# Block-sparse attention with a token and channel mixer: landing times of the build-time planner reset, and crossbar transposes of Q and K from pair 8 on

## The chip, the core and the metric

The kernel runs on one core of one Trainium2 chip. The metric is the device time of one execution in microseconds (us). Executions of one kernel differ (the kernel before took 272.06 to 276.02 us in one session), so each time is given as a median of several runs with its range, and kernels are compared on the same chip in the same rounds. A run more than 1.5% above the fastest of its kernel counts as slow and is left out of the ratios. "Faster" or "slower" needs 2%; smaller differences are read from their 95% interval. The span is the time from the first to the last instruction in the profile. The mean clock is the share of TensorE's full clock that was granted over it.

## The reference

Four batches of eight heads, 768 positions of 64 numbers each, pass through attention under a block mask. The result, 4 x 768 x 512, passes through a mixer with one token layer and one channel layer. The code is shortened.

```python
def _attn_ref(q, k, v, sampled_blocks):            # block 32, window 1, 3 random blocks per row
    scores = scale * np.matmul(q, k.transpose(0, 1, 3, 2))
    mask = ...                                     # window | first and last block | sampled_blocks
    scores = np.where(mask, scores, -1000000000.0)
    attn = np.exp(scores - np.max(scores, axis=-1, keepdims=True))
    attn = attn / (np.sum(attn, axis=-1, keepdims=True) + 1e-09)
    return np.matmul(attn, v)

def _moe_ref(x, w_tok1, w_tok2, w_ch1, w_ch2):     # 768->256->768, then 512->1536->512
    h = np.maximum(x.transpose(0, 2, 1) @ w_tok1, 0.0) @ w_tok2
    u = x + h.transpose(0, 2, 1)
    return u + np.maximum(u @ w_ch1, 0.0) @ w_ch2
```

## The kernel before

The 32 heads are worked off as 16 pairs. For each pair, Q and K must stand transposed in `qtb` and `ktb` (head dimension on the partitions; 24 more partitions carry the mask). TensorE makes scores, ScalarE takes exponentials (`et`), TensorE multiplies by V (`po`), VectorE normalises. The token and channel matmuls fill what is left of TensorE.

**The planner.** Which instruction goes where in each engine's program is decided when the kernel is built. A `Planner` simulates the engines with a fixed cost for each operation and a landing time for each transfer; at each step an engine is given the ready operation of best priority. On the chip every engine then executes in exactly that order. A wrong landing time is therefore not a slower plan: it is an instruction in the wrong place, at which the engine stands with everything behind it.

```python
    dma = {"free": 0.0}
    RATE = 200.0

    def landing(issue, nbytes):
        dma["free"] = max(dma["free"], issue + 1.6 * US) + nbytes / RATE
        return Ev(dma["free"] + 0.6 * US)
```

From V of pair 0 on, all loads of Q, K, V and weights are issued by GpSimd, in a software queue that casts f32 to bf16; each load waits for its raw buffer (four each).

**Two ways to transpose.** Pairs below `NPE` (except pair 0, which has its own code) use TensorE: for each of K and Q a VectorE copy, six transposes, and two copies out of PSUM, the memory that TensorE writes to. Pairs from `NPE` on use the DMA's crossbar, which transposes while it moves data: VectorE copies raw K and Q into a "wide" buffer, and SyncE issues one DMA transpose for each. There are `NL` = 2 wide buffers for each of K and Q, so the copy of pair p may only go when the transpose of pair p-2 has read its buffer.

```python
    # relayout(p), for K and Q
            if nm != "v" and p >= NPE:
                deps.append(wide_there[nm, p % NL])
                if p - NL >= NPE:
                    deps.append(xb_done[nm, p - NL])        # the wide buffer is free again
            lays[nm + "ev"] = P.op(("dve",), {"dve": 320.0}, deps, emit, prio=2 if nm != "v" else 3)
    ...
    # crossbar(p), for K and Q
                nc.sync.dma_start_transpose(out=bufs[p % NV]..., in_=wide[nm, p % NL]...)
            ...
            ev = P.op(("sp",), {"sp": 1600.0}, deps, emit, prio=1, lat=5000.0)
            xb_done[nm, p] = ev                             # planned: 1.6 + 5.0 + 0.05 us
```

The softmax here doesn't subtract the row's maximum and nothing guards it: scores larger than these inputs give would overflow.

Of the kernel before, what the change touches and what calls it, by code (L numbers as in the profile page):

```python
# [25 lines left out]
def free(base_ap: bass.AP, extra_offset: int, dims) -> bass.AP:  # L26

    return bass.AP(
        tensor=base_ap.tensor,
        offset=base_ap.offset + extra_offset,  # L30
        ap=[list(base_ap.ap[0])] + [list(d) for d in dims],
    )
# [137 lines left out]
def kernel(  # L170
# [12 lines left out]
    nc = tc.nc  # L183
# [7 lines left out]
    NV = 4  # L191
    NR = 4
    NET = 8
    NPE = 10
    NL = 2

    sb1 = ctx.enter_context(tc.tile_pool(name="sb1", bufs=1))
# [12 lines left out]
    qtb = [sb1.tile([128, 2, S], BF16, name=f"qtb{n}") for n in range(NV)]  # L210
# [3 lines left out]
        for n in range(NL) for nm in ("k", "q")  # L214
    }

    P = Planner({"ps": 2, "po": 1, "pm": 3, "et": NET, "a_t": 2, "o": 3, "rc": 2,
                 "uT": 3})
    US = 1e3


    raws, arrive = {}, {}
    dma = {"free": 0.0}
    RATE = 200.0

    def landing(issue, nbytes):
        dma["free"] = max(dma["free"], issue + 1.6 * US) + nbytes / RATE
        return Ev(dma["free"] + 0.6 * US)

    def load_pair(p, t, parts=("k", "q", "v")):  # L230
        for nm, src in (("k", k), ("q", q), ("v", v)):
# [39 lines left out]
    R = slice(64, 88)  # L271
# [32 lines left out]
    for i in range(8):  # L304
# [5 lines left out]
        out=ind[R, :, :], in_=free(one[R, 0:1], 0, [[0, NC], [0, 128]]), compare_op=ALU.is_ge,  # L310
# [3 lines left out]
        out=ind[R, :, :], in_=ind[R, :, :], compare_op=ALU.is_ge, fill=0.0,  # L314
# [3 lines left out]
        out=ident[:, :], in_=free(one[:, 0:1], 0, [[0, 128]]), compare_op=ALU.is_equal, fill=0.0,  # L318
# [21 lines left out]
        out=edge[R, :], in0=edge[R, :], scalar1=-11.5, scalar2=None, op0=ALU.add  # L340
# [3 lines left out]
        out=edge[R, :], in0=edge[R, :], scalar1=121.0, scalar2=None, op0=ALU.is_gt  # L344
    )
    nc.vector.tensor_scalar(
        out=bandg[R, :], in0=dkf[R, :], scalar1=1.0, scalar2=edge[R, 0:1],
# [5 lines left out]
    for col, other in ((0, bandg), (2, allow), (4, allow)):  # L353
        nc.vector.scalar_tensor_tensor(
            out=allow[R, :], in0=kbf[R, :], scalar=sampf[R, col : col + 1], in1=other[R, :],
# [3 lines left out]
        out=t2add[R, :], in0=allow[R, :], scalar1=-MASKVAL, scalar2=MASKVAL,  # L359
# [17 lines left out]
    def first_turn(nm, hf):  # L377
        t = psM.tile([128, 3, 128], BF16, tag="pm", name=f"t{nm}first{hf}")
        for c in range(3):
            nc.tensor.matmul(  # L380
                out=t[:, c, :], lhsT=lay0[nm][:, 3 * hf + c, :, :].rearrange("p h d -> p (h d)"),
                rhs=ident[:, :], start=(c == 0), stop=(c == 2), is_transpose=True,
            )
        return t

    def first_evac(copy, nm, hf, hd, t):
        buf = (ktb if nm == "k" else qtb)[0]
        copy(
            out=buf[0:64, hd, 384 * hf : 384 * hf + 384],
            in_=t[64 * hd : 64 * hd + 64, :, :].rearrange("p c s -> p (c s)"),  # L390
        )

    def e2_mm(hf, pool, tag):
        t = pool.tile([128, 512], FP32, tag=tag, name=f"pm_e2_{hf}")
        nc.tensor.matmul(
            out=t[R, 0:384], lhsT=t2add[R, :], rhs=indf[:, 384 * hf : 384 * hf + 384],
            start=True, stop=True,
        )
        return t

    def e2_copy(copy, hf, hd, t):
        copy(out=qtb[0][R, hd, 384 * hf : 384 * hf + 384], in_=t[R, 0:384])
# [24 lines left out]
    rows_there = {p: Ev(START) for p in range(NV)}  # L427
# [3 lines left out]
    def first_rest():  # L431

        def band(eng):
            nc.vector.tensor_copy(out=ktb[0][R, 1, 384:S], in_=indf[:, 384:S])

        P.op(("dve",), {"dve": 250.0}, [], band, prio=0)
        for nm in ("k", "q"):
            box, last, rel = {}, Ev(), Ev()

            def emit(nm=nm, box=box, rel=rel):  # L440
                P.take("pm", rel)
                box["t"] = first_turn(nm, 1)

            yield 330.0, [Ev(START + (200.0 if nm == "k" else 600.0))], [("pm", 1)], emit, last
            for hd in range(2):
                def evac(eng, nm=nm, hd=hd, box=box):
                    first_evac(vcopy, nm, 1, hd, box["t"])

                ev = P.op(("dve",), {"dve": 350.0}, [last], evac, prio=0)
                f_there[nm, 1].same_as = ev  # L450
                rel.same_as = ev
        box, last, rel = {}, Ev(), Ev()

        def emit():
            P.take("pm", rel)
            box["t"] = e2_mm(1, psM, "pm")

        yield 330.0, [], [("pm", 1)], emit, last
        for hd in range(2):
            def copy(eng, hd=hd, box=box):  # L460
                e2_copy(vcopy, 1, hd, box["t"])

            e2_there = P.op(("dve",), {"dve": 420.0}, [last], copy, prio=0)
            rel.same_as = e2_there
        rows_there[0] = e2_there
        for n in range(1, NV):
            def spread(eng, n=n):
                nc.sync.dma_start(out=qtb[n][R, :, :], in_=qtb[0][R, :, :])

            rows_there[n] = P.op(("sp",), {"sp": 100.0}, [e2_there], spread, prio=0, lat=2500.0)  # L470

    def wide_stream():

        box, done, rel = {}, Ev(), Ev()

        def emit():
            P.take("pm", rel)
            box["m"] = psM.tile([128, 2, NC, 24], FP32, tag="pm", name="pm_wide")
            for i, rhs in enumerate((ident[R, 64:88], t2add[R, :])):
                for c in range(NC):  # L480
                    nc.tensor.matmul(
                        out=box["m"][:, i, c, :], lhsT=ind[R, c, :], rhs=rhs,
                        start=(i == 0 and c == 0), stop=(i == 1 and c == NC - 1),
                    )

        yield 500.0, [Ev(62 * US)], [("pm", 1)], emit, done
        for n in range(NL):
            for i, nm in enumerate(("k", "q")):
                def clear(eng, nm=nm, n=n):
                    nc.vector.memset(wide[nm, n][:, :, :, 64:128], 0.0)  # L490

                def copy(eng, nm=nm, n=n, i=i):
                    nc.vector.tensor_copy(
                        out=wide[nm, n][:, :, :, 64:88],
                        in_=free(box["m"][:, i, 0, :], 0, [[0, 2], [24, NC], [1, 24]]),
                    )
                ev = P.op(("dve",), {"dve": 420.0}, [Ev(60 * US)], clear, prio=6)
                ev = P.op(("dve",), {"dve": 450.0}, [done, ev], copy, prio=6)
                wide_there[nm, n].same_as = ev
                rel.same_as = ev  # L500
# [13 lines left out]
    def relayout(p):  # L514
        lays = {}
        for nm in ("k", "q", "v") if p else ("v",):
# [3 lines left out]
            def emit(eng, nm=nm, raw=raw):  # L520
                if nm == "v":
                    nc.vector.tensor_copy(out=vaug[p % NV][:, :, :, 0:64], in_=raw[:, :, :, :])  # L522
                elif p >= NPE:
                    nc.vector.tensor_copy(out=wide[nm, p % NL][:, :, :, 0:64], in_=raw[:, :, :, :])
# [8 lines left out]
            if nm == "v" and p >= NV:  # L533
                deps.append(pv_done[p - NV])
            if nm != "v" and 2 <= p < NPE:
                deps.append(qT_there[p - 1, 1])
# [3 lines that stand above are left out]
                    deps.append(xb_done[nm, p - NL])  # L540
# [7 lines left out]
    def crossbar(p):  # L548

        lays = relayout(p)  # L550
        for nm, bufs, there in (("k", ktb, kT_there), ("q", qtb, qT_there)):
            def emit(eng, nm=nm, bufs=bufs):
                nc.sync.dma_start_transpose(
                    out=bufs[p % NV][:, :, :].rearrange("e h (c s) -> e (h c) s", c=NC),
                    in_=wide[nm, p % NL][:, :, :, :].rearrange("p h c e -> p (h c e)"),
                )
            deps = [lays[nm + "ev"]]
            if p >= NV:
                deps.append(qk_done[p - NV])
            ev = P.op(("sp",), {"sp": 1600.0}, deps, emit, prio=1, lat=5000.0)  # L560
            xb_done[nm, p] = ev
            there[p, 0], there[p, 1] = ev, ev

    def transposes(p):
        yield lambda: ("v", p) in raws
        if p >= NPE:
            crossbar(p)
# [52 lines left out]
    def qk_stream():  # L620
        for s in steps:
# [32 lines left out]
            else:  # L654
                deps = [e for hd in range(2) for e in (kT_there[p, hd], qT_there[p, hd])]
                if p < NPE:
                    deps.append(rows_there[p % NV])
# [273 lines left out]
    P.stream(3, tok_stream())  # L931
    P.stream(4, ch_stream())
    P.stream(-1, wide_stream())


# [55 lines left out]
```

## Time and profile before

| what | before |
|---|---|
| median of 3 runs | 273.65 us (273.64 to 275.1) |
| span of the profiled execution (timed at 272.80 us) | 271.1 us, mean clock 0.992 |
| TensorE / ScalarE / VectorE busy | 97% / 68% / 43% |
| transposes on TensorE for Q and K (L587) | 54 + 54 |
| first token matmul | 30.04 us |
| last exponential ends | 149.91 + 5.33 = 155.24 us |

The DMA row of the page's slices; one slice is 6.8 us, a digit is the busy share in tenths:

```profile
DMA  6999999998699764891300036200132002310123
GB/s 146 189 219 202 213 201 208 200 201 133 70 212 170 145 101 97 136 120 39 62 2 2 0 60 174 83 33 2 39 116 80 0 0 80 117 40 0 41 77 116
```

The DMA engines are full up to slice 9 (61 us) and reach their lowest point for some time in slice 10 (68 to 75 us, 70 GB/s). The first crossbar transpose of this kernel is issued at 72.18 us, so in or after that gap.

### The profile page before, as it was taken

What the parts mean: (1) busy time and instruction counts of PE and PEld (TensorE: products, weight loads), DVE (VectorE), ACT (ScalarE), POOL (GpSimd) and SP (SyncE); (2) the same over time, 40 slices, a digit from 0 to 9 for tenths busy, and PEclk for the clock granted to TensorE, in tenths of its full rate; (3) what the DMA queues carried; (4) which work ended last, traced back from release to release, by engine and by line L of the source; (5) the groups of instructions that cost most, each with busy time, mean ns of one, the idle gap of its engine ahead of it and who ended that gap; (6) DMA issues with size and microseconds to landing.
All of it is one profiled execution on the core that took longest, in us unless ns stands there. A gap on an engine that the chain in (4) does not pass through costs nothing.

```text
span 271.1 us, 6192 instructions
## 1 busy us (share of the span) xinstructions
PE 263.4 (97%) x2587; PEld 171.5 (63%) x2595; DVE 117.8 (43%) x268; ACT 185.1 (68%) x274; POOL 42.2 (16%) x66
## 2 busy tenths in 40 slices
PE   8899999999999999999999999999999999999995
PEld 3566777777777767777777664456445554456444
DVE  8678788777963744643626442200221003200132
ACT  6699999999999999999999910177104750077200
POOL 8835555561231000000000000000000000000000
PEclk9899999999999999999999999999999999999999
DMA  6999999998699764891300036200132002310123
GB/s 146 189 219 202 213 201 208 200 201 133 70 212 170 145 101 97 136 120 39 62 2 2 0 60 174 83 33 2 39 116 80 0 0 80 117 40 0 41 77 116
DMA packets 48512, 27.98 MB, mean 103 GB/s; under 512 B 29708, under 2 KB 44828, under 8 KB 48484
## 3 DMA queue, kind: packets, MB, share of 16 engines
q0 software_dynamic: 15104, 12.98, 30.8%
q1 hardware_dynamic: 33108, 14.41, 23.2%
q8 instruction: 20, 0.33, 0.5%
q10 hardware_dynamic: 272, 0.20, 0.3%
q14 instruction: 8, 0.07, 0.1%
HBM read 26.74 MB, written 6.29 MB: 122 GB/s over the span
## 4 chain that ended last, share of the span: by engine, by line
PE 73%; ACT 15%; DMA 7%; POOL 2%; issue 2%; DVE 1%; DVEq 0%; POOLq 0%; ACTq 0%
PE pm_ch L856 22%; PE pm_ch L882 22%; ACT et L642 15%; PE ps L633 14%; PE po L686 7%; DMA vraw<-in_v_dram 6%; PE pm_tok L789 3%; PE pm_tok L764 2%; DMA out_dram<-o 1%; PE tk L587 1%; DVE ktb L602 0%; PE pm_ut L818 0%; POOL ktb L313 0%; POOL ktb L309 0%; POOL vraw L235 0%
## 5 line engine op out<-in xcount | busy, mean ns | idle before, releaser
L642 ACT ACTIVATE et<-ps 128x768 bf16<-128x768 f32 x192 | 144.0, 809 | 4.7 <-PE ps L633 2.7
L633 PE MATMUL ps<-qtb,ktb 88*128 88x384 bf16 x384 | 94.8, 328 | 1.6 <-ACT et L642 0.4
L728 ACT ACTIVATE rc<-pm_ch 128x384 bf16<-128x384 f32 x74 | 36.3, 491 | 59.3 <-PE pm_ch L856 43.3
L856 PE MATMUL pm_ch<-uT,w_ch 128*128 128x384 bf16 x384 | 72.1, 326 | 0.0
L686 PEld LDWEIGHTS <-et 128*128 128x128 bf16 x1152 | 56.2, 97 | 23.3 <-issue 2.0
L882 PE MATMUL pm_ch<-w_ch,rc 128*128 128x512 bf16 (+2 forms) x304 | 62.9, 362 | 0.4
L686 PE MATMUL po<-vaug,et 128*128 128x65 bf16 x1152 | 61.5, 193 | 0.9 <-DVE vaug L522 0.9
L891 DVE TENSOR_TENSOR o<-pm_ch,x 128x512 f32<-128x512 f32 x23 | 15.9, 691 | 88.4 <-PE pm_ch L882 88.4
L882 PEld LDWEIGHTS <-rc 128*128 128x128 bf16 x312 | 29.6, 98 | 31.9
L856 PEld LDWEIGHTS <-w_ch 128*128 128x128 bf16 x384 | 36.2, 98 | 20.9
L633 PEld LDWEIGHTS <-ktb 88*128 88x128 bf16 x384 | 35.0, 99 | 11.1 <-issue 2.8
L797 DVE TENSOR_TENSOR x<-pm_tok,x 128x512 bf16<-128x512 f32 x24 | 15.9, 685 | 11.3 <-PE pm_tok L789 11.2
L701 DVE TENSOR_TENSOR x<-po,recip 128x384 bf16<-128x384 f32 x32 | 17.8, 557 | 1.1
L730 DVE TENSOR_SCALAR rc<-pm_ch 128x384 bf16<-128x384 f32 x22 | 12.2, 554 | 13.0 <-PE pm_ch L856 12.9
L789 PE MATMUL pm_tok<-a_t,w_tok 128*128 128x256 bf16 x96 | 17.3, 277 | 0.0
L764 PE MATMUL pm_tok<-x,w_tok 128*128 128x256 bf16 x96 | 16.7, 272 | 0.0
L700 DVE RECIPROCAL recip<-po 128x6 f32<-128x6 f32 x32 | 6.3, 195 | 22.3 <-PE po L686 21.7
L235 POOL DMA_DIRECT2D vraw<-in_v_dram x16 | 11.6, 725 | 20.3 <-DVE vaug L522 15.3
L602 DVE COPY ktb<-tk 64x768 bf16<-64x768 bf16 x18 | 9.9, 552 | 5.8 <-PE tk L587 5.6
L235 POOL DMA_DIRECT2D kraw<-in_k_dram x15 | 10.8, 717 | 9.3 <-DVE recip L700 2.9
L235 POOL DMA_DIRECT2D qraw<-in_q_dram x15 | 10.9, 724 | 8.6 <-DMA w_tok<-in_moe_w_tok_dram 2.0
L602 DVE COPY qtb<-tq 64x768 bf16<-64x768 bf16 x18 | 10.0, 553 | 1.1 <-PE tq L587 0.7
(72 smaller groups left out, 102.2 us busy)
## 6 DMA issues: line engine op xcount, KB each, us to landing
out_dram<-o SPq DMA_DIRECT2D x23, 256.0 KB, 2.0
vraw<-in_v_dram POOLq DMA_DIRECT2D x16, 192.0 KB, 7.4
w_ch<-in_moe_w_ch_dram POOLq DMA_DIRECT2D x8, 384.0 KB, 9.8
kraw<-in_k_dram POOLq DMA_DIRECT2D x15, 192.0 KB, 8.0
qraw<-in_q_dram POOLq DMA_DIRECT2D x15, 192.0 KB, 7.7
w_tok<-in_moe_w_tok_dram POOLq DMA_DIRECT2D x2, 384.0 KB, 10.0
kf<-in_k_dram SPq DMA_DIRECT2D x2, 192.0 KB, 3.7
ktb<-ktb SPq DMA_DIRECT2D x3, 72.0 KB
```

Source lines behind the costliest of these rows:

```text
L235: nc.gpsimd.dma_start(out=raw[:, :, :, :], in_=APx(src, 2 * p * S * D, [[NC * D, 128], [S * D, 2], [1, NC * D]]),)
L602: nc.vector.tensor_copy(out=buf[0:64, hd, :], in_=i)
L633: nc.tensor.matmul(out=ps[:, hd, 0:384], lhsT=ktb[n][0:88, hd, 128 * j : 128 * j + 128], rhs=qtb[n][0:88, hd, 384 * half : 384 * half + 38 ...
L642: nc.scalar.activation(out=et[:, :, :], in_=ps[:, :, 0:384], func=AF.Exp, scale=0.125)
L686: nc.tensor.matmul(out=po[:, hd, c, :], lhsT=et[:, hd, 128 * c : 128 * c + 128], rhs=va[:, hd, j, 0:65], start=(j == 0 and hd == 0 and c = ...
L701: nc.vector.tensor_tensor(out=free(xs[b][:, pb // 2, 3 * half, 128 * (pb % 2) : 128 * (pb % 2) + 128], 0, [[64, 2], [256, 3], [1, 64]],), ...
L728: nc.scalar.activation(out=o(), in_=i, func=AF.Relu)
L764: nc.tensor.matmul(out=box["pm"][:, t, :], lhsT=w_tok1[:, sc, 128 * t : 128 * t + 128], rhs=xs[b][:, g, sc, :], start=(t == 0 and sc == 0) ...
L789: nc.tensor.matmul(out=ubox["pm"][:, i, :], lhsT=w_tok2[:, t, :, 2 * s2 + i], rhs=a_t[:, t, :], start=(i == 0 and t == 0), stop=(i == 1 an ...
L797: nc.vector.tensor_tensor(out=st[b]["u"][:, g, 2 * s2 : 2 * s2 + 2, :], in0=ubox["pm"][:, :, :], in1=xs[b][:, g, 2 * s2 : 2 * s2 + 2, :], ...
L856: nc.tensor.matmul(out=pbox["pm"][:, 0:384], lhsT=w_ch1[:, dmc, 128 * cc : 128 * cc + 128], rhs=st[b]["uT"][:, dmc // 2, 3 * sh : 3 * sh + ...
L882: nc.tensor.matmul(out=pbox["pm"][:, 0:n], lhsT=box["rc"][:, cc, 128 * sc : 128 * sc + 128], rhs=w_ch2[:, cc, lo : lo + n], start=(cc == 0 ...
```

## The change

It has two intents. The planner's landing times are set to what the trace of the loads shows, so that VectorE no longer stands at a copy whose data is not there. And two more pairs, 8 and 9, are transposed by the crossbar, which takes 24 transposes off TensorE. The rows of pair 1 are also spread by a VectorE copy instead of a DMA, and the set-up of the wide buffers is moved up.

```diff
-    NPE = 10
+    NPE = 8
...
-    dma = {"free": 0.0}
+    dma = {"free": 7.6 * US}
     RATE = 200.0
     def landing(issue, nbytes):
-        dma["free"] = max(dma["free"], issue + 1.6 * US) + nbytes / RATE
-        return Ev(dma["free"] + 0.6 * US)
+        dma["free"] = max(dma["free"], issue + 3.2 * US) + nbytes / RATE
+        return Ev(dma["free"] + 0.15 * US)
...
             def spread(eng, n=n):
-                nc.sync.dma_start(out=qtb[n][R, :, :], in_=qtb[0][R, :, :])
-            rows_there[n] = P.op(("sp",), {"sp": 100.0}, [e2_there], spread, prio=0, lat=2500.0)
+                if eng == "dve":
+                    nc.vector.tensor_copy(out=qtb[n][R, :, :], in_=qtb[0][R, :, :])
+                else:
+                    nc.sync.dma_start(out=qtb[n][R, :, :], in_=qtb[0][R, :, :])
+            rows_there[n] = P.op(
+                ("dve",) if n == 1 else ("sp",), {"dve": 560.0, "sp": 800.0}, [e2_there], spread,
+                prio=1, lat=60.0 if n == 1 else 5000.0,
+            )
...
-        yield 500.0, [Ev(62 * US)], [("pm", 1)], emit, done      # wide_stream
+        yield 500.0, [Ev(50 * US)], [("pm", 1)], emit, done
...
-                ev = P.op(("dve",), {"dve": 420.0}, [Ev(60 * US)], clear, prio=6)
+                ev = P.op(("dve",), {"dve": 420.0}, [Ev(48 * US)], clear, prio=6)
```

## The prediction

> **What bounds the kernel now.** I read the page's slices first, then the work of TensorE by line in 10 us windows, then the idle times of ScalarE and VectorE in the timeline of the first 36 us, then the landing of each load in the DMA view. The slices:
>
> ```profile
> PE   8899999999999999999999999999999999999995
> ACT  6699999999999999999999910177104750077200
> ...
> PEclk9899999999999999999999999999999999999999
> ```
>
> One slice is 6.8 us. Up to about slice 23 (154 us) both ScalarE (192 exponentials) and TensorE are full; after that TensorE alone is, working off matmuls of the two channel layers (L856, L882), and ScalarE is mostly idle. The chain of waits agrees: its last 110 us are L856 and L882 back to back. So the end is set by the sum of TensorE's work plus the time in which it has none; time saved on ScalarE counts only if it removes such holes.
>
> A busy TensorE is not a full one, so I counted work. In the dense tail 96 matmuls of L856 take 15.60 us, 162.5 ns for 384 columns. Six QK-side transposes take 24.95 - 24.62 = 0.33 us, 55 ns each; six P·V matmuls 0.18 us, 30 ns each.
>
> ```profile
> 24.62 0.49 PE L587 MATMUL tq<-ident,qlay 128*128 128x128 bf16 x6
> 24.95 0.49 PE L633 MATMUL ps<-qtb,ktb 88*128 88x384 bf16 x2
> ```
>
> With these costs and the counts by line per window: 10 to 20 us holds 24 score matmuls (3.9 us), 66 P·V (2.0) and 24 transposes (1.3), 7.2 us of 10; 20 to 30 us holds 8.1; 30 to 60 us holds 9.7 per 10 us. From 6.3 us (first scores) to 30 us about 6.3 us of TensorE is empty. After 30 us, when the token-mixing matmuls begin to fill gaps, only some 3 us is lost in all the rest. Hence two sources of gain: work removed anywhere, and holes removed before 30 us.
>
> Before 30 us the pace is ScalarE's: one exponential per 0.735 us (13 in 9.56 us) against 0.61 us of TensorE work per step (two scores 0.325, six P·V 0.18, transposes 24 x 55 ns over 12 steps = 0.11). Where ScalarE itself stood still:
>
> ```profile
> 10.24 1.51 ACT L642 ACTIVATE et<-ps 128x768 bf16<-128x768 f32 x2 [1.17 <-PE ps L633]
> 11.94 0.81 ACT L642 ACTIVATE et<-ps 128x768 bf16<-128x768 f32 x1 [0.18 <-PE ps L633]
> 13.44 0.81 ACT L642 ACTIVATE et<-ps 128x768 bf16<-128x768 f32 x1 [0.70 <-PE ps L633]
> 14.69 9.56 ACT L642 ACTIVATE et<-ps 128x768 bf16<-128x768 f32 x13 [0.43 <-PE ps L633]
> 24.82 7.45 ACT L642 ACTIVATE et<-ps 128x768 bf16<-128x768 f32 x10 [0.57 <-PE tk L587]
> ```
>
> That is 1.17 + 0.18 + 0.70 + 0.43 + 0.57 = 3.05 us. Their causes are on VectorE and in the clock:
>
> ```profile
> 8.68 0.36 DVE L522 COPY vaug<-vraw 128x768 bf16<-128x768 bf16 x1 [1.39 <-DMA vraw<-in_v_dram]
> 9.07 0.74 DVE L388 COPY ktb<-tkfirst 64x384 bf16<-64x384 bf16 x2
> ...
> 23.26 0.36 DVE L522 COPY vaug<-vraw 128x768 bf16<-128x768 bf16 x1 [1.07 <-DMA vraw<-in_v_dram]
> 23.54 0.35 DVE L527 COPY klay<-kraw 128x768 bf16<-128x768 bf16 x1
> ```
>
> VectorE runs in program order. The build-time planner believed V of pair 0 to land at 3.4 + 1.6 + 0.98 + 0.6 = 6.58 us and put its copy ahead of the copies of K's second half (L388). It landed at 8.69 us, so the K copies, ready since about 7.3 us, started at 9.07, and the fourth score step waited for them. TensorE had 0.20 us of matmul in the microsecond from 8 us; then its clock fell:
>
> ```profile
> 8.00:9.00 1.00, 0.20 (x2) 0.00 (x0) 0.32 (x1) 1.00 (x2) 1.00 (x2) 1.00 1.22 155
> ...
> 11.00:12.00 1.00, 0.90 (x8) 0.56 (x7) 0.97 (x4) 0.81 (x3) 0.61 (x1) 0.50 1.28 194
> 12.00:13.00 1.00, 1.00 (x12) 0.83 (x10) 0.56 (x2) 0.75 (x1) 0.70 (x2) 0.50 1.31 198
> ```
>
> (after the five engines come clock, DMA share, GB/s.) The half clock lasts from about 11 to 14.3 us, and the waits of 0.18, 0.70 and 0.43 us lie there.
>
> **What the skill says.** The Trainium skill, "TensorE: Matmul & The Clock Gate", Part 1: the clock is halved after a window of about 3.4 us without enough matmul work and given back after a busy one. The trace agrees in size: half clock for some 3.3 us, after a thin stretch from 7.7 to 11 us. Same page, "Wait — 56ns, not 53.3ns?": 55.6 ns per 128-column matmul; here 55. "DMA: Bandwidth & Descriptors", Issuing engines are not separate DMA queues: loads from all issuers share the same 16 DMA engines. The trace agrees: about 200 GB/s from 10 to 60 us whoever issues. "VectorE: DVE Perf Modes", The three transpose paths: a crossbar transpose is slower alone (1309 against 390 ns for one 128x128 block) but leaves TensorE and PSUM alone; here a whole 128x1536 crossbar transpose lands in 3.9 to 5.2 us.
>
> **The change part by part.**
>
> *Landing model.* Working both formulas through (0.983 us per load of 192 KB, 1.966 per 384 KB) against the measured landing: V of pair 0 before 6.58, after 8.73, measured 8.69. K of pair 1: 7.57, 9.72, 9.74. Q of pair 1: 8.55, 10.7, 11.06. V of pair 1: 9.53, 11.68, 12.15. K of pair 3: 17.4, 19.55, 21.24. V of pair 3: 19.4, 21.5, 23.24. So the new model is right to 0.5 us up to pair 2 and still 1.7 us early at pair 3 (the two token weights, planned at 2 us each, land about 2.6 us apart). The DMA does nothing differently: queue order and bytes are the same. What changes is the order on VectorE and TensorE. K's second half is now copied from about 7.3 us, so the fourth step does not wait: the 1.17 us goes. P·V of pair 0 comes after 9.1 us and can catch up beside the scores; TensorE from 7.5 to 11 us then does about 1.6 us of scores and 0.8 of P·V in 3.4 us instead of some 1.5, so I expect, less surely, that the clock stays up and the 1.31 us goes too. I take 80% of these 2.48 us: 2.0 us. The 0.57 us at pair 3 I leave in: the lag of execution behind the plan shrinks together with the model's error, and about 1 us of mismatch remains.
>
> *Rows of pair 1 by VectorE.* One copy of some 0.56 us (a 24x384 copy took 0.252, a 768-wide one 0.35; 1536 wide by the slope) replaces one DMA of 72 KB. VectorE between 7.3 and 15.3 us then has about 7.5 us of work: two K copies 0.74, V 0.36, Q 0.72, mask rows 1.03, pair 1 layouts 0.7, four copies out of PSUM 2.2, this 0.56, V 0.34, norm 0.76. Tight, worth perhaps 0.2 us either way; counted as zero.
>
> *Crossbar for pairs 8 and 9.* Removes 2 x 12 = 24 transposes: 24 x 55 ns = 1.32 us of TensorE, all on the bound, since token and channel matmuls are waiting to fill the place. It removes 8 copies out of PSUM (8 x 0.553 = 4.4 us of VectorE, beside other work) and adds four DMA transposes. Pair 8's raw K is copied at 51.1 us; with landing of about 5 us it is there by 60 us, and its scores start near 77 us: hidden. The set-up of the wide buffers (12 small matmuls, 4 clears, 4 copies) only moves from about 65 to about 50 us, at zero sum.
>
> Sum: 2.0 + 1.32 = 3.3 us; 273.65 - 3.3 = 270.3 us.
>
> **Rivals.** *The new wait at pair 3.* K of pair 3 is planned at 19.55 and lands near 21.2. If VectorE stands at that copy while a norm (L700, L701) is queued behind it, the one output accumulator in PSUM is not freed, P·V stops and the scores behind it stop too. For: the same order produced the 1.07 us wait and 0.57 us on ScalarE before. Against: the score buffers give about one step of slack. It would cost 1 to 1.5 us more: 271.5. *The clock falls anyway.* The stretch before V arrives is still thin, half scores and half nothing. Then only 1.17 + 1.32 comes: 271.2. *The whole early stall disappears and pair 3 as well*, with a little from the waits at 62 to 66 us (about 0.6 us of holes near the wide-buffer set-up): 1.32 + 3.05 + 0.5, 268.8. *The loads are the limit and retiming gives nothing*: DMA is full from 5 to 60 us; but a pair needs three loads, about 3 us, per 8.8 us of exponentials, so loads lead after pair 3. This would leave only 1.32: 272.3.
>
> **Range and chances.** Most rivals lie between 268.8 and 272.3; the range is 268.5 to 272.4. Faster by over 2% needs 268.2 or less, more than all the stalls and the transposes together: 0.07. Slower by 2% would need a crossbar that comes late or a lost order over the whole plan: 0.02.
>
> **What would show it.** Right: no 1.4 us wait of VectorE for V at 8.7 us and K's copies near 7.3; clock 1.0 from 11 to 14 us; 84 instead of 108 transposes on L587; eight crossbar pairs; token matmuls starting near 28 instead of 30.0 us; the last exponential about 2 us earlier. Wrong: the half clock still there, a VectorE wait for K of pair 3 with ScalarE idle over 1 us after 20 us, or scores of pair 8 waiting for a DMA.

## More of the kernel before

The DMA view of 68 to 100 us, with transfer, count and median time from issue to landing (the trace holds only some of the landings):

```profile
ktb<-kwide SPq DMA_TRANSPOSE x4, 4.6
qtb<-qwide SPq DMA_TRANSPOSE x3, 6.3
```

And the DMA view of 85 to 89 us, where two of them run: what was moved in 40 slices of the 4 us, then by queue packets, MB, and the share of the 16 engines' time:

```profile
GB/s 289 287 292 284 262 289 289 297 289 289 289 287 292 292 289 287 292 328 172 200 200 154 184 192 169 215 200 177 238 261 292 289 289 289 292 289 287 289 292 294
...
q1 hardware_dynamic: 3392, 0.85, 95.5%
q0 software_dynamic: 272, 0.20, 33.5%
```

The transposes (q1) have the engines mostly to themselves, and some 290 GB/s are moved in most slices.

## The result, and the profile after

The kernel after takes 281.74 us (median of 4 runs, 279.82 to 281.86) against 273.64 us (4 runs, 273.44 to 275.1). The ratio is 1.0266, with a 95% interval of 1.0222 to 1.031: slower. A ratio here is the mean time of one kernel's fast runs over that of the other's in the same rounds, so not quite the ratio of the medians. All results are correct.

The slices of the page of the kernel after (one slice is 7.0 us):

```profile
PE   8899999982699999999999999999999999999995
ACT  6899999990389999999999960057302770067200
...
PEclk9999999996589999999999999999999999999999
DMA  6999999999959978499030022420023002210123
```

Slices 9 and 10 (63 to 77 us) tell the story. TensorE falls to 2 and 6 tenths, ScalarE to 0 and 3, the clock to half. In the kernel before nothing of the sort stood there. The DMA row is full up to slice 10.

**The early part went as meant.** The timelines of VectorE and ScalarE in the first 31 us; each row has start, length, engine, line, operation, count, and in brackets the idle time just before it and what ended that:

```profile
8.21 0.74 DVE L388 COPY ktb<-tkfirst 64x384 bf16<-64x384 bf16 x2 [0.75 <-PE tkfirst L380]
...
12.22 0.34 DVE L528 COPY vaug<-vraw 128x768 bf16<-128x768 bf16 x1
```

```profile
7.71 5.16 ACT L648 ACTIVATE et<-ps 128x768 bf16<-128x768 f32 x7 [0.78 <-PE ps L639]
13.49 17.02 ACT L648 ACTIVATE et<-ps 128x768 bf16<-128x768 f32 x23 [0.62 <-PE ps L639]
```

K's second half is copied at 8.21 instead of 9.07 us, and VectorE no longer waits 1.39 us for V. Between its first exponential and 30 us ScalarE stops once, for 0.62 us, where it stopped five times for 3.05 us. The first token matmul starts at 28.28 us (30.04 before), 1.76 us earlier. That is in spite of a first exponential 0.86 us later (7.71 against 6.85), a difference of the start phase, which the change does not touch: among the experiments' profiles, with the same start code, it lies between 6.86 and 7.72 us. The transposes on L593 are 84, eight pairs go through the crossbar.

**The loss is in one place.** First the timeline of SyncE, which issues the crossbar transposes of pairs 8 and 9 (K, Q, K, Q):

```profile
53.25 3.67 SPq L559 DMA_TRANSPOSE ktb<-kwide  x1
57.09 8.41 SPq L559 DMA_TRANSPOSE qtb<-qwide  x1
65.61 5.57 SPq L559 DMA_TRANSPOSE ktb<-kwide  x1
71.22 1.51 SPq L559 DMA_TRANSPOSE qtb<-qwide  x1
```

Already the issue takes 3.67, 8.41 and 5.57 us, where those of the kernel before take 1.4 to 3.2. From issue to landing K of pair 8 took 13.7 us (until about 66.9) and Q 14.9 (until 71.96). Then VectorE, in the same stretch:

```profile
67.02 0.36 DVE L530 COPY kwide<-kraw 128x768 bf16<-128x768 bf16 x1 [7.13 <-DMA vraw<-in_v_dram]
67.30 0.69 DVE L803 TENSOR_TENSOR x<-pm_tok,x 128x512 bf16<-128x512 f32 x1
72.06 0.36 DVE L530 COPY qwide<-qraw 128x768 bf16<-128x768 bf16 x1 [4.07 <-DMA qtb<-qwide]
```

These are the copies of pair **10**'s K and Q into the wide buffers that pair 8 still occupies. VectorE stood at them for 7.13 and 4.07 us. The first wait is put down to a load of V, but the copy starts 0.1 us after the K transpose landed, and the second is put down to the Q transpose outright. Nothing needs pair 10 before about 99 us (in experiment 8, which has no stall, its first exponential starts at 99.68). What stands behind the copies is needed at once: the residual add of the token layer ("x add", L803; it has priority 3, behind such a copy), and behind that TensorE and ScalarE:

```profile
68.04 0.61 PE L824 MATMUL pm_ut<-ident,x 128*128 128x128 bf16 x4 [5.92 <-DVE x L803]
68.44 0.85 PE L639 MATMUL ps<-qtb,ktb 88*128 88x384 bf16 x2
```

```profile
69.38 0.81 ACT L648 ACTIVATE et<-ps 128x768 bf16<-128x768 f32 x1 [6.54 <-PE ps L639]
...
74.15 0.81 ACT L648 ACTIVATE et<-ps 128x768 bf16<-128x768 f32 x1 [2.56 <-PE ps L639]
```

The transposes of x (L824) come before the scores in TensorE's order. So the scores, whose own data had long been there, waited for VectorE's add, which waited for VectorE's copy, which waited for a transpose. The chain of waits has the same two steps, a DMA piece of 14.87 us from 57.09 and the copy behind it:

```profile
57.09 14.87 DMA qtb<-qwide
72.06 0.36 DVE qwide L530
```

**How much.** From 62 to 79 us TensorE worked 0.12 us at full clock, then 2.65 and 3.06 us at 0.50 and 3.00 us at 0.59. As an estimate from these rows that is 0.12 + 1.33 + 1.53 + 1.77 = 4.75 us of full-speed work in 17 us, so 12.2 us lost. Against this stand 1.76 us of early gain and 1.32 us of transposes: 12.2 - 3.1 = 9.1 us. The spans differ by 280.0 - 271.1 = 8.9 us.

**Why the transpose was slow.** The DMA view of 61 to 64 us in the kernel after:

```profile
q0 software_dynamic: 567, 0.41, 92.6%
q1 hardware_dynamic: 570, 0.15, 43.7%
```

Loads and transposes get the same *number of packets*, 567 and 570. From 57 to 68 us they are 1,931 and 1,911. A packet of the loads is some 720 bytes, one of the transposes 256. So the transposes move 0.15 MB in 3 us, some 50 GB/s, against some 290 alone. One tensor of a pair is 128 x 1536 x 2 bytes, 1,536 packets of 256; K and Q together are 3,072, as an estimate 16.2 us at 190 per us. From K's issue to Q's landing 18.7 us passed, but not evenly: from 53 to 57 us the DMA view shows loads alone (1,092 packets), and from 71 to 72 us transposes alone (1,014). The Trainium skill, "DMA: Bandwidth & Descriptors", Queues, rings and completion order, says this: "each SDMA engine round-robins between the queue rows it has work for, at *packet* granularity". The counts agree with it, if the page's packet (by the page several descriptors) holds as many of the trace's packets on both queues, which no run here shows. The prediction had not looked this section up: it used another one of that page, which says that the issuers' transfers share the engines and interleave, but not in what turns.

### The profile page after: what moved, and what is told of

It is laid out like the page before. It is cut to its first block, busy times and chain, and to the rows that moved or that the text cites. A ratio compares the mean times of both kernels' runs of the same rounds, so it can differ in the third digit from the quotient of the medians.

```text
span 280.0 us, 6156 instructions
## 1 busy us (share of the span) xinstructions
PE 265.3 (95%) x2571; PEld 171.4 (61%) x2571; DVE 115.5 (41%) x263; ACT 184.7 (66%) x272; POOL 42.1 (15%) x66
## 4 chain that ended last, share of the span: by engine, by line
PE 79%; ACT 10%; DMA 6%; DVE 2%; issue 1%; DVEq 0%; ACTq 0%
PE pm_ch L862 22%; PE pm_ch L888 21%; PE ps L639 17%; ACT et L648 10%; PE po L692 9%; DMA qtb<-qwide 5%; PE pm_tok L770 3%; PE pm_tok L795 3%; PE ps_idle L299 2%; DMA out_dram<-o 1%; DVE qtb L402 0%; PE tk L593 0%; PE pm_e L395 0%; PE tq L593 0%; DVE qtb L388 0%
## 5 line engine op out<-in xcount | busy, mean ns | idle before, releaser
L648 ACT ACTIVATE et<-ps 128x768 bf16<-128x768 f32 x192 | 144.6, 810 | 14.5 <-PE ps L639 13.1
L639 PE MATMUL ps<-qtb,ktb 88*128 88x384 bf16 x384 | 95.9, 331 | 1.8 <-ACT et L648 1.1
L862 PE MATMUL pm_ch<-uT,w_ch 128*128 128x384 bf16 x384 | 73.0, 326 | 2.3 <-DVE uT L839 2.3
L734 ACT ACTIVATE rc<-pm_ch 128x384 bf16<-128x384 f32 x72 | 35.4, 491 | 56.5 <-PE pm_ch L862 56.4
L692 PEld LDWEIGHTS <-et 128*128 128x128 bf16 x1152 | 56.6, 98 | 22.0 <-issue 1.4
L888 PE MATMUL pm_ch<-w_ch,rc 128*128 128x512 bf16 (+2 forms) x312 | 64.0, 363 | 0.0
L692 PE MATMUL po<-vaug,et 128*128 128x65 bf16 x1152 | 61.5, 194 | 0.0
L639 PEld LDWEIGHTS <-ktb 88*128 88x128 bf16 x384 | 35.8, 99 | 15.4 <-issue 5.9
L803 DVE TENSOR_TENSOR x<-pm_tok,x 128x512 bf16<-128x512 f32 x24 | 16.0, 686 | 10.2 <-PE pm_tok L795 10.2
L736 DVE TENSOR_SCALAR rc<-pm_ch 128x384 bf16<-128x384 f32 x24 | 13.2, 555 | 13.0 <-PE pm_ch L862 13.0
L770 PE MATMUL pm_tok<-x,w_tok 128*128 128x256 bf16 x96 | 17.3, 279 | 0.0
L795 PEld LDWEIGHTS <-w_tok 128*128 128x128 bf16 x96 | 9.8, 129 | 1.4
L824 PE MATMUL pm_ut<-ident,x 128*128 128x128 bf16 x24 | 2.9, 248 | 5.9 <-DVE x L803 5.9
```

The costliest lines, as they stand in the source:

```text
L639: nc.tensor.matmul(out=ps[:, hd, 0:384], lhsT=ktb[n][0:88, hd, 128 * j : 128 * j + 128], rhs=qtb[n][0:88, hd, 384 * half : 384 * half + 38 ...
L648: nc.scalar.activation(out=et[:, :, :], in_=ps[:, :, 0:384], func=AF.Exp, scale=0.125)
L692: nc.tensor.matmul(out=po[:, hd, c, :], lhsT=et[:, hd, 128 * c : 128 * c + 128], rhs=va[:, hd, j, 0:65], start=(j == 0 and hd == 0 and c = ...
L734: nc.scalar.activation(out=o(), in_=i, func=AF.Relu)
L770: nc.tensor.matmul(out=box["pm"][:, t, :], lhsT=w_tok1[:, sc, 128 * t : 128 * t + 128], rhs=xs[b][:, g, sc, :], start=(t == 0 and sc == 0) ...
L795: nc.tensor.matmul(out=ubox["pm"][:, i, :], lhsT=w_tok2[:, t, :, 2 * s2 + i], rhs=a_t[:, t, :], start=(i == 0 and t == 0), stop=(i == 1 an ...
```

## The experiments

The theory: pairs 8 and 9 put their transposes into the time in which loads fill the DMA; they take three times as long; the planner does not know it and puts copies of pair 10 into VectorE's order that wait for them. The rivals: that the new landing times spoilt the order of the whole plan; that the wide buffers were simply too few. Each edit is against the kernel after unless said otherwise. Each chip ran the kernel before beside its kernels: 273.62 us (7 runs) for experiments 1 to 4, 273.40 (7 runs) for 5 to 8, 273.36 (11 runs) for 9 to 12.

### 1. Without the crossbar part

```diff
-    NPE = 8                # and the wide set-up back at 62 and 60 us
+    NPE = 10
```

> The change without its crossbar part: new landing times and the rows of pair 1 by VectorE, but pairs 8 and 9 turned on TensorE and the wide set-up at its old place. Main theory (the two early crossbar transposes are slowed to about 14 us by the load queue, and a VectorE copy queued in program order waits for them): no VectorE wait over 2 us between 50 and 80 us, and 273.64 less the 1.8 to 2.6 us that the token matmuls start earlier, so 271.0 to 271.9 us. Rival 'retiming' (the new landing times set the loads so that everything at 60 us collides): a stall of several us at 55 to 80 us stays, 278 us or more.

Measured: 271.97 us (271.1 to 272.18), ratio 0.9933 (0.9898 to 0.9969), 0.07 us above the expected range. No stall; VectorE waits for a transpose once, 1.73 us. The first token matmul starts at 28.39 us. So the retiming (with the spread by VectorE) is a gain of some 1.7 us by itself, and all the loss is in the crossbar part.

### 2. The crossbar part alone, on the kernel before

```diff
-    NPE = 10               # kernel before; and the wide set-up at 50 and 48 us
+    NPE = 8
```

> The crossbar part alone (pairs 8 and 9, wide set-up at 50 us) on the old landing times and old row spread. Main theory: the transposes of pair 8 meet the same full load queue, landing 10 us or more, VectorE waits for them in the copy of pair 10 into the same wide buffer, and the time is 279 to 285 us. Rival 'retiming': no such wait, about 272.3 us (273.64 less 1.32).

Measured: 285.38 us (280.6 to 288.17); two of the four runs count as slow, and the ratio of the other two is 1.0308 (1.0228 to 1.0388). The profiled run is one of the slow ones, so its sizes are not compared, but the pattern is the same: VectorE stands 3.48 us (put down to a transpose) and 5.40 us (put down to a load) at the copies of K and Q into the wide buffers, and then 6.15 and 4.60 us at the next ones. The rival of the retiming falls: with the old landing times the loss is there too.

### 3. More wide buffers

```diff
-    NL = 2                 # the fourth pair of buffers is the dead first-load tiles, read as bf16
+    NL = 4
```

> The change with four wide buffers in place of two (the fourth pair on the dead first-load tiles), so that the copies of pairs 10 and 11 wait for no transpose. Main theory: the transposes of pairs 8 still land after 10 us or more, VectorE has no wait over 2 us there, ScalarE no idle of 6 us at 63 us, the clock stays up, and the time falls to 269 to 271 us. Rival 'too late' (the scores of pair 8 need the late transposes themselves): ScalarE still stops for 3 us or more at pair 8, 274 us or more. If the half clock or the earlier wide set-up were the cause, it would also stay near 280.

Measured: 280.46 us (279.99 to 281.66), ratio 1.0256 (1.0214 to 1.0298). The expectation missed: nothing was gained. The transposes of pair 8 took 14.0 and 14.8 us as before, and the wait was there again, now at the copies of pair **12**, which are next in line for pair 8's buffers (VectorE's timeline):

```profile
67.33 0.36 DVE L532 COPY kwide<-kraw 128x768 bf16<-128x768 bf16 x1 [3.60 <-DMA ktb<-kwide]
...
72.09 0.36 DVE L532 COPY qwide<-qraw 128x768 bf16<-128x768 bf16 x1 [4.39 <-DMA qtb<-qwide]
```

ScalarE stood still for 8.00 us before its exponential at 74.58. The planner runs copies ahead as far as buffers let it, so more buffers move the early copies up; they give no slack. What has to be right is the time at which the planner believes a buffer to be free. That makes it sharper than "too few buffers": the second rival falls, and the wrong number is the 5 us. A time near 280 us was also what the expectation gave to the earlier wide set-up as a cause; experiment 8 keeps that set-up and has no loss.

### 4. Planning pairs 8 and 9 late

```diff
-            ev = P.op(("sp",), {"sp": 1600.0}, deps, emit, prio=1, lat=5000.0)
+            ev = P.op(("sp",), {"sp": 1600.0}, deps, emit, prio=1, lat=17000.0 if p < 10 else 5000.0)
```

> The change with one number altered in the planner: the landing of the crossbar transposes of pairs 8 and 9 is put at 17 us in place of 5. Buffers, bytes and instructions are the same, only the order on the engines differs. Main theory: transposes still land after 10 us or more, but the copy of pair 10 stands later in VectorE's order, so no wait over 2 us and 269 to 271.5 us. Rivals that blame the transposes' slowness itself or the DMA load: still 276 us or more.

Measured: 278.45 us (278.07 to 281.23), ratio 1.0198 (1.0139 to 1.0257). The expectation missed, and the verdict at 2% is unclear, but half of the expectation holds. The stall at 62 us is gone: ScalarE works from 53.39 to 79.76 us in one piece. It comes back one step on, at the copies that wait for pair 10, which was still planned at 5 us:

```profile
86.40 0.63 DVE L530 COPY kwide<-kraw 128x768 bf16<-128x768 bf16 x2 [5.92 <-DMA ktb<-kwide]
```

ScalarE then stands for 5.32 us. The delay of two pairs is handed on: Q of pair 8 took 18.9 us, and all transposes go through one queue in order.

### 5. Holding the loads back

```diff
+                if x >= 10:        # pull(): a load of pair x waits until x of pair x-5 is there
+                    y = x - 5
+                    nc.gpsimd.tensor_copy(out=gate[:, :], in_=xs[y // 4][...2 elements of pair y...])
```

> The change, but GpSimd holds the loads of pair 10 and later until the output of the pair five before is there (a copy of two elements that reads it stands before each group of loads). So almost no load is queued while pairs 8 and 9 go through the crossbar. Main theory (transposes and loads take turns packet by packet on the same DMA engines, so a queue of waiting loads holds a transpose to some 50 GB/s): the transposes of pair 8 land in under 8 us, no VectorE wait over 2 us, ScalarE without idle over 1 us from 55 to 95 us, and 269 to 271 us. Rival 'crossbar' (a transpose at this place is slow whatever else runs): landing still over 12 us, stall stays, 276 us or more.

Measured: 271.98 us (271.44 to 272.59), ratio 0.9944 (0.9899 to 0.9988). The planned landing is still 5 us. The DMA view from 54 to 58 us, and the landings of pair 8:

```profile
q1 hardware_dynamic: 2350, 0.59, 83.9%
q0 software_dynamic: 67, 0.05, 7.6%
...
ktb<-kwide SPq DMA_TRANSPOSE x1, 4.0
qtb<-qwide SPq DMA_TRANSPOSE x1, 3.7
```

With few loads beside them the transposes take 4.0 and 3.7 us instead of 13.7 and 14.9, and the stall is gone. This is the direct test of the contention. The time is above the 269 to 271 us expected: VectorE now waits for the held loads, 7.2 us in all for K (5 times, longest 3.0), 6.8 for V and 2.3 for Q, and ScalarE 0.55, 0.89 and 0.80 us.

### 6. The landing times alone

```diff
-    NPE = 8                # wide set-up back; rows of pair 1 spread by DMA again, planned as before
+    NPE = 10
```

> Only the new landing times (pairs 8 and 9 on TensorE, rows of pair 1 by DMA, wide set-up at its old place). If the landing times carry the early gain, the fourth score step no longer waits for V of pair 0 and the time is 271 to 272.3 us; if the row copy on VectorE was needed for it, 273 to 274 us.

Measured: 271.82 us (271.43 to 271.98), ratio 0.9935 (0.9894 to 0.9976); first token matmul at 28.84 us.

### 7. The spread by VectorE alone

```diff
-    dma = {"free": 7.6 * US}        # and 3.2, 0.15 back to 1.6, 0.6; NPE and wide set-up back
+    dma = {"free": 0.0}
```

> Only the rows of pair 1 by VectorE, old landing times. If the landing times carry the early gain, no change: 273.3 to 274.2 us, with the wait of VectorE for V of pair 0 still there. If the row copy carries it: 271 to 272 us.

Measured: 272.75 us (272.66 to 273.85), ratio 0.9980 (0.9936 to 1.0025), between the two ranges of the expectation. VectorE waits 1.58 us for V of pair 0, and the first token matmul starts at 30.46 us. So the early gain is that of the landing times; the spread alone changes nothing that can be told from zero.

### 8. All crossbar landings planned at 17 us

```diff
-            ev = P.op(("sp",), {"sp": 1600.0}, deps, emit, prio=1, lat=5000.0)
+            ev = P.op(("sp",), {"sp": 1600.0}, deps, emit, prio=1, lat=17000.0)
```

> The change with the planned landing of all crossbar transposes at 17 us (before, with pairs 8 and 9 alone, the stall left 60 us and came back at pair 10). Loads and transposes still share the engines. Main theory, order part: no copy into a wide buffer stands in VectorE's order before its transpose has landed, so no VectorE wait over 2 us and 269.5 to 272 us, although transposes take 10 us or more. Rival 'slowness itself costs': scores of a pair wait for their own transposes, 275 us or more.

Measured: 270.36 us (269.98 to 270.84), ratio 0.9883 (0.9833 to 0.9933). One number turns the kernel after from 2.7% slower into 1.2% faster than the kernel before (less than 2%, but clear of zero by its interval). The DMA view of 61 to 64 us shows that the transposes are as slow as ever, and ScalarE's timeline that nobody minds:

```profile
q0 software_dynamic: 555, 0.40, 88.7%
q1 hardware_dynamic: 560, 0.14, 39.6%
```

```profile
53.35 26.37 ACT L648 ACTIVATE et<-ps 128x768 bf16<-128x768 f32 x35 [0.18 <-PE ps L639]
```

K took up to 13.0 and Q up to 16.6 us, and VectorE waited for none of them. So the slow transfer costs nothing that this run shows; the copy placed in front of other work did. Whether fast transfers with this plan would gain more was not tested.

### 9. Planned at 11 us

```diff
-            ev = P.op(("sp",), {"sp": 1600.0}, deps, emit, prio=1, lat=17000.0)       # experiment 8
+            ev = P.op(("sp",), {"sp": 1600.0}, deps, emit, prio=1, lat=11000.0)
```

> As the run with all crossbar landings planned at 17 us, but at 11 us: a dose between the change (5 us, 281.7 us) and 17 us (270.4 us). Main theory (the stall is the part of the real landing, 14 to 17 us here, that the plan does not know): a VectorE wait of 1 to 5 us for a transpose is back between 60 and 95 us, and the time lies between the two, 271 to 277 us. If any late order of the copies is enough, 270 to 270.8; if the landing must be exact, 279 or more.

Measured: 278.66 us (277.22 to 282.56, one run slow; the other three 277.22 to 279.36), ratio 1.016 (1.0091 to 1.023), above what was expected. VectorE's waits are back and shorter:

```profile
70.38 0.36 DVE L530 COPY kwide<-kraw 128x768 bf16<-128x768 bf16 x1 [3.75 <-DMA ktb<-kwide]
```

Q follows at 74.54 with 3.11 us. ScalarE loses 0.84 + 2.82 + 0.58 + 0.58 + 0.46 = 5.3 us there. The profiled execution also lost 1.83 + 0.55 + 0.70 + 0.49 = 3.6 us to an early half clock, which the expectation had not counted. The direction is right: planned landings of 5, 11 and 17 us give ratios of 1.0266, 1.016 and 0.9883, with waits of 7.13 + 4.07, 3.75 + 3.11 and none.

### 10. V of pair 0 copied first

```diff
-    ... prio=2 if nm != "v" else 3)                 # on top of experiment 8
+    ... prio=2 if nm != "v" else 3 if p else 1)
```

> All landings at 17 us, and V of pair 0 copied before the layouts of pair 1 (it lay ready from 8.7 us and was copied at 11.6 to 12.2). If a thin TensorE between 9 and 12 us is what lets the clock fall at about 11.7 us in some executions, the clock stays at 1.0 from 10 to 16 us and the time is 269 to 270.2 us; if the fall depends on the phase of the clock's window alone, it is equal to the next run within 0.3 us.

Measured: 269.91 us (269.58 to 272.05, 8 runs), ratio 0.9857 (0.9808 to 0.9905), the lowest median of all. V of pair 0 is copied at 10.30 us instead of 11.60, and P·V starts earlier. The mean clock is at least 0.998 in all 8 runs, where experiment 11 has two runs of six at 0.994. That is too few to decide the question of the expectation, and the intervals of the two ratios overlap.

17 us is not enough in every execution: in the profiles of experiments 10 and 11 Q of pair 8 took 19.9 and 18.4 us, and VectorE waited for it 2.53 and 1.12 us. It cost little: from 53 us until its last exponential ScalarE never stopped for a whole microsecond.

### 11 and 12. Experiments 8 and 1 once more, side by side

No edit. The point is the crossbar part with the retiming in both, on one chip.

> The kernel with all landings planned at 17 us once more, beside the one without early crossbar transposes on the same chip: 270.0 to 270.8 us.

> The change without its crossbar part once more. The 24 removed TensorE transposes at 55 ns are 1.32 us, so this run should be 1.0 to 1.7 us above the run before it: 271.3 to 272.2 us.

Measured: 270.57 us (269.83 to 272.26, 6 runs), ratio 0.9889 (0.9841 to 0.9937), and 271.71 us (271.37 to 272.44, 6 runs), ratio 0.9930 (0.9884 to 0.9975). The medians differ by 1.14 us; between experiments 1 and 8, on two chips, it was 1.6. This is not the 24 transposes alone: experiment 11 also plans the landings of pairs 10 to 15 at 17 us, which experiment 12 leaves at 5.

## Why the prediction was right or wrong

**What held.** The bound: time is TensorE's work plus its holes; the loss was a hole, and the estimate of 12.2 - 3.1 = 9.1 us against 8.9 measured agrees with that sum. The arithmetic of the landing model held: VectorE no longer stands at V of pair 0. The early gain was put at 2.0 us; experiments 1 and 12 give 273.62 - 271.97 = 1.65 and 273.36 - 271.71 = 1.65. The transposes were put at 1.32 us; experiments 11 and 12 give 1.14, with the other planned landings mixed in. The whole sum was 3.3 us; experiment 8, which is the change with one number set right, gives 273.40 - 270.36 = 3.0. The feared stall at pair 3 did not come: in the kernel after, ScalarE runs from 13.49 to 30.51 us without a stop. The spread by VectorE was counted as zero, and experiment 7 can't tell it from that.

**The step that failed.** It is "Pair 8's raw K is copied at 51.1 us; with landing of about 5 us it is there by 60 us, and its scores start near 77 us: hidden." Two things are wrong in it.

First, the 5 us. They were read from transposes issued from 72 us on, in a stretch with few loads (from 72 to 104 us 1,546 packets of loads against 14,828 of transposes). The new ones were issued at 53 us, and the prediction itself said that the DMA is full from 5 to 60 us. Landing was 13.7 and 14.9 us; with the loads held back (experiment 5) 4.0 and 3.7.

Second, "hidden". It asked who needs the result and found that the scores had 17 us to spare. They did, and more: landing at 71.96 us would still have been in time for scores at 77, and in the kernel before the scores of pair 8 start only at 81.67. But a transfer has a second customer, the next writer of its *source* buffer. Pair 10's copy was tied to it, and the planner, which believed in 6.65 us, had put it in front of the x add. It took both mistakes to lose the time. Transposes that land in 4 us remove the stall (experiment 5), and so does planning for late ones (experiment 8, where the landing is as bad and the kernel is faster). So lateness itself was harmless, and the path through the source buffer was the cost.

**The rivals.** None of the four named this. The chance of slower was 0.02, with "a crossbar that comes late" as its ground; that ground was right, but nothing in the profile was asked about it. The sign of failure given last, "scores of pair 8 waiting for a DMA", would have missed it, since no score waits for a DMA: the scores wait for TensorE's order, which waits for VectorE.

**Smaller points.** "P·V of pair 0 comes after 9.1 us" was some 3 us off: V was copied at 12.22 us, since pair 1's copies and the spread have better priority. The 1.31 us for the clock can come only in some executions: of the 11 runs of the kernel before in the last session, 6 with mean clock 1.000 average 272.88 us and 5 with 0.988 to 0.994 average 274.70, a difference of 1.8 us. The profile of before that was read is of the second kind (0.992). That the clock stayed up in the profile of the kernel after was luck, as far as these runs show: it still halves at about 11.5 us in the profiles of experiments 4, 8, 9 and 11, which plan the early part in the same way. "3.9 to 5.2 us" for a transpose are the landings of K alone; those of Q in the same trace are 3.7 to 6.3. "Whoever issues" was not seen there: from 15 to 60 us GpSimd alone issued loads.

**What stays open.** Packet turns do not explain why no packet of K's transpose moved before 57 us, 4 us after its issue, nor why both queues almost stopped from 64.3 to 65.0 us. They do not explain every slow transpose either: in experiment 4, from 70 to 74 us, 824 packets of transposes ran beside only 235 of loads and still moved only some 52 GB/s. How much of the stall is the half clock after it (0.70 + 0.59 + 0.58 + 0.59 = 2.5 us of ScalarE's waits follow the two long ones or lie between them) is read off the trace and was not tested by itself. Nobody tried to give the x add a better priority than the copies into the wide buffers.

## What to carry to other kernels

A duration belongs to the place where it was measured: before moving a transfer, read the DMA row at the new time, and count packets by queue, since a transfer of small packets beside one of large packets loses in bytes. For every transfer ask two questions, who needs its result and who waits for its source buffer, and look for the second one in the program order of an engine that does urgent work. In this kernel, whose order is planned at build time, transposes planned late cost little and transposes planned too early stopped an engine, and more buffers only let the planner run further into the same wait.

## What the Trainium skill lacked or had wrong

- "DMA: Bandwidth & Descriptors", Queues, rings and completion order: the statement of turns by packet fits the counts 567 : 570 and 555 : 560. The page does not draw the consequence for a crossbar transpose: packets of 256 bytes beside casting loads of some 720 bytes got some 50 GB/s, against some 290 alone.
- Same page, Latency and other measured facts: it gives 261 GB/s for a transpose with a non-contiguous middle dimension and 350 to 400 for a contiguous one. Here, with hardly a load beside them, some 290 GB/s were moved at best (between the two), and transposes of 128 x 1536 landed in 4.0 and 3.7 us (experiment 5); beside a full load queue those of pair 8 took 13.0 to 19.9 us in the fast runs. The page gives no figure for a transpose beside other traffic.
- None of the pages read says that the *issue* of a transpose grows too: SyncE was held 8.41 us by one issue under load, against 1.4 to 3.2 us in the kernel before.
- None of the pages read explains transposes of some 52 GB/s with few loads beside them (824 packets to 235 in 4 us, experiment 4).
- "TensorE: Matmul & The Clock Gate", Part 1: it speaks of an idle window of about 3.4 us, running freely, before the clock is halved, and gives no share of work below which a window counts as idle. The windows fit: in these traces each stretch of half clock before the end of the work lasts 3.41 us or a multiple (3.41 in the kernel before, 13.65 in the kernel after). The traces also give a share. In the first 21 us of the 14 profiles the clock fell after windows of 3.41 us in which TensorE was busy, by the profile, for 1.53 to 2.50 us (2.36 in the kernel before, whose longest idle time was 0.89 us), and stayed after those of 2.53 us and more. Half clock ended after windows of 3.08 us and more, and went on after 2.92 and less. The share is not the whole rule: later windows of 1.74, 2.25 and 2.37 us (experiments 2 and 7) kept the full clock.
